# Linear attention, 32 heads: GpSimd sums the seven odd tiles 3 to 15 of phi(k) instead of tiles 10 to 14, and takes its relu of k whole, behind the memset of ones

## Chip, core and metric

The kernel runs on one core of one Trainium2 chip. The metric is the device time of one execution in microseconds (us); a smaller time is better.

## What is computed

There are 32 heads; in each, q, k and v are 2048 x 128 in bf16. Cut to what matters:

```python
phi_q = where(q > 0, q + 1, exp(q)) + 1e-6
phi_k = where(k > 0, k + 1, exp(k)) + 1e-6
kv  = einsum("bhsd,bhse->bhde", phi_k, v)      # 128 x 128 a head
z   = einsum("bhsd->bhd", phi_k)
num = einsum("bhqd,bhde->bhqe", phi_q, kv)
den = einsum("bhqd,bhd->bhq", phi_q, z)[..., None] + 1e-6
return num / den
```

The kernel writes phi(x) as a sum of two parts, min(exp(x), 1) + 1e-6 and max(x, 0). A matrix product with phi can so be made as two products, one with each part, that add up in PSUM, or as one product when some engine has added the parts before.

## The kernel before

**Data of a head.** The 2048 rows of a head are 16 tiles of 128 rows; partition p holds rows 16p to 16p + 15, and tile j is the 128 columns from 128 j. k, v and q come in by one 512 KB transfer each on SP's queue (L380) into six buffers each, and the output leaves by one (L590). `emk` (L401) and `emq` (L487) are the min-exp parts, `rk` (L391) and `rq` (L473 on ScalarE, L475 on VectorE) the relu parts; each has three buffers.

**Work of each engine for one head h in the steady part (h from 3 on).**

- ScalarE: exp of k (`ek`, L387), exp of the transposed q (`eq`, L466), relu of half of the transposed q (L473), and the copy of the summed kv and z out of PSUM (`kvs`, L449).
- VectorE, in this order in each turn: the denominators of a head (`den`, L525), their reciprocals (L531), a last tile (L536) and the divisions (L543, twice), then the other half of relu of q (L475), `emk` (L401) and `emq` (L487).
- GpSimd, in this order in each turn: `add` (L409), which adds the `emk` part to `rk` in place for the tiles in `ADD`, so that `rk` holds phi(k) there; the first half of relu of k of the next head (L391, tiles 0 to 7); the memset of ones (L445); the second half of that relu (L391, tiles 8 to 15).
- TensorE, in this order in each turn: for one head the first 2 of 5 groups of the numerators (`num`, L502 and L503); then the odd tiles of kv (`kv2`, L447) of the next head; then the other 3 groups of `num`; then the transposes of q (L455) and the even tiles of kv (L440 and L442) of the head after that.

**How kv takes its tiles.** A tile in `ADD` takes one product, with `rk`, which then holds the sum; another takes two, one with `emk`, one with `rk` (L426 and L427). An even tile (other than 0) is 128 columns of v wide and has a product one column wide for z with it (L436, recorded at L339); an odd tile is 129 wide, because the memset of ones has by then written 1 into the column of v ahead of it, the last column of the even tile before (L445). So the memset of head h waits until TensorE has read the even tiles of h, and the odd tiles wait for the memset.

**What sets the order.** Each operation is added to a plan with an engine and a key; each engine runs its own in order of the key, and the plan turns reads and writes into waits on semaphores. The keys that matter here: `add` of head h stands on GpSimd at h + 0.5, the memset of h at h + 0.6 (L445), the relu of k of head h at h - 0.45 and h (L398 and L399). `add` of head h reads `emk` and `rk` of h, and by its argument `more` it also waits until `emq` of head h - 1 is done (L421), the operation that VectorE runs right after `emk` of h:

```python
add("pool", h + 0.5, ADD, "phik",
    more=[("emq", (h - 1) % 3)] + ([("phik", 1)] if h == 2 else []))
```

On TensorE the even tiles are two operations: the even tiles outside `ADD` (L440), and behind them the even tiles in `ADD` (L442), which wait for `add`. `num` waits until VectorE's divisions of the head before have freed its PSUM groups, the first two groups by the first division and the rest by the second. The relu of q on VectorE waits until ScalarE's `eq` of that head is done. Heads 0 to 2 are a start of their own: head 0 is summed on VectorE whole, head 1 on VectorE for its even tiles 4 to 14 (L416) and for the odd tiles in `ADD` (L417), and relu of k is one whole instruction for heads 0 and 2 on GpSimd and for head 1 on VectorE (L396).

Of the kernel before, what the change touches and what calls it, by code (L numbers as in the profile page):

```python
# [12 lines left out]
def _ap(base: bass.AP, elem_offset: int, dims):  # L13
    return bass.AP(base.tensor, base.offset + elem_offset, [list(base.ap[0])] + [list(d) for d in dims])
# [217 lines left out]
def bass_standalone__linear_attn_elu__prompt_kernel(  # L232
# [18 lines left out]
    LAST = NH - 1  # L251
    SLOW = {LAST - 3: (16, 48)}

    ADD = (10, 11, 12, 13, 14)
    EVEN, ODD = tuple(range(0, NT, 2)), tuple(range(1, NT, 2))
    MORE = (4, 6, 8, 10, 12, 14)
    GAP = 32
# [7 lines left out]
    with ExitStack() as es:  # L265
# [39 lines left out]
        pl = Plan()  # L305

        def rows(x, h):
# [11 lines left out]
                                                     base=0, pattern=[[-1, P]], channel_multiplier=1),  # L319
               reads=[("id0",)], writes=[("ident",)])  # L320
# [17 lines left out]
        def mm_held(pe, out_ap, rhs, stop, start=False):  # L338
            return pe.add_instruction(mybir.InstMatmult(  # L339
                start_tensor_calc=start, stop_tensor_calc=stop, ldweights=False, bass_skip_group_check=True,  # L340
                tile_position=(0, 0), tile_size=(P, P), name=nc.get_next_instruction_name(), engine=mybir.EngineType.PE,
                ins=[pe.lower_ap(rhs), pe.lower_ap(held[0])], outs=[pe.lower_ap(out_ap)]))
# [27 lines left out]
        for h in range(NH):  # L370
            def at(name, key, h=h):
                return place.get((name, h), h + key)

            bi, b2, b3, bo = h % NBI, h % 2, h % 3, h % NBO

            def load(name, buf, src, key, h=h, bi=bi):
                dst, rws = buf[:, bi], rows(src, h)
                if name == "v":
# [9 lines left out]
                   reads=[("k", bi)], writes=[("ek", b2)])  # L388
            def relu_k(eng, key, parts, h=h, bi=bi, b3=b3):
                c = slice(parts[0] * HALF, (parts[-1] + 1) * HALF)  # L390
                pl.add(eng, key, lambda e: e.tensor_scalar(rk_sb[:, b3, c], k_sb[:, bi, c], BIG, 0.0, op0=ALU.min, op1=ALU.max),  # L391
                       reads=[("k", bi)] + ([("rk", h - 1, 1)] if 0 < h < 3 else []),
                       writes=[(n, b3, p) for p in parts for n in ("rk", "rkx")] + [("phik", b3), ("phix", b3)], kind="rk")

            if h < 3:
                relu_k("dve" if h == 1 else "pool", at("rk", 0), (0, 1))  # L396
            else:
                relu_k("pool", h - 0.45, (0,))  # L398
                relu_k("pool", h, (1,))  # L399
            pl.add("dve", at("emk", -3 + 0.95),  # L400
                   lambda d, b2=b2, b3=b3: d.tensor_scalar(emk_sb[:, b3, :], ek_sb[:, b2, :], 1.0, EPS, op0=ALU.min, op1=ALU.add),  # L401
                   reads=[("ek", b2)], writes=[("emk", b3)], kind="emk")

            def add(eng, key, tiles, name, b3=b3, more=()):
                step = tiles[1] - tiles[0]

                def f(e):
                    a, b = (_ap(x[:, :, :], b3 * NT * D + tiles[0] * D, [[step * D, len(tiles)], [1, D]]) for x in (rk_sb, emk_sb))
                    return e.tensor_tensor(out=a, in0=a, in1=b, op=ALU.add)  # L409
                pl.add(eng, key, f, reads=[("emk", b3), ("rkx", b3, 0), ("rkx", b3, 1)] + list(more), writes=[(name, b3)], kind=name)  # L410

            if h == 0:
                add("dve", -2.04, range(NT), "phik")
                both_of, one_of = (), range(NT)
            elif h == 1:
                add("dve", -1.89, MORE, "phix")  # L416
                add("dve", -1.88, tuple(j for j in ADD if j in ODD), "phik")  # L417
                both_of, one_of = tuple(j for j in EVEN if j not in MORE), MORE
            else:
                add("pool", h + 0.5, ADD, "phik",  # L420
                    more=[("emq", (h - 1) % 3)] + ([("phik", 1)] if h == 2 else []))  # L421
                both_of, one_of = (tuple(j for j in EVEN if (j in ADD) == x) for x in (False, True))

            def kv(pe, tiles, start=False, stop=False, h=h, bi=bi, b3=b3, both_of=both_of):
                for j in tiles:
                    both = j in both_of or (j in ODD and j not in ADD and h > 0)  # L426
                    for src in (emk_sb, rk_sb) if both else (rk_sb,):  # L427
                        first, fin = start and j == tiles[0] and src is (emk_sb if both else rk_sb), stop and j == tiles[-1] and src is rk_sb
                        w = src[:, b3, j * D:(j + 1) * D]
                        l = j == 0 or (j in ODD and h > 0)  # L430
                        c = GAP + j * D
                        last = pe.matmul(kvz_ps[:, 1 - l:NC], lhsT=w, rhs=v_sb[:, bi, c - l:c + D], start=first, stop=fin,  # L432
                                         skip_group_check=True)
                        if not l:
                            held[0] = w
                            last = mm_held(pe, kvz_ps[:, 0:1], ones_sb[:, 0:1], fin)  # L436
                return last
            base = [("v", bi), ("vo", bi), ("ones",), ("vones",)]
            if h:
                pl.add("pe", at("kv", -1.2), lambda pe, kv=kv, t=both_of: kv(pe, t, start=True),  # L440
                       reads=[("emk", b3), ("rk", b3, 0), ("rk", b3, 1)] + base, writes=[("bankkv",)])
            pl.add("pe", at("kv", -1.199), lambda pe, kv=kv, t=one_of, f=h == 0: kv(pe, t, start=f, stop=f),  # L442
                   reads=[("phix" if h == 1 else "phik", b3)] + base + ([] if h else [("first",)]), writes=[("bankkv",)])
            if h:
                pl.add("pool", h + 0.6, lambda g, bi=bi: g.memset(_ap(vfull, bi * VW + GAP + D - 1, [[2 * D, NT // 2], [1, 1]]), 1.0),  # L445
                       reads=[("v", bi)], writes=[("vo", bi)], kind="vo")
                pl.add("pe", at("kv2", -0.2985), lambda pe, kv=kv: kv(pe, ODD, stop=True),  # L447
                       reads=[("phik", b3), ("emk", b3), ("rk", b3, 0), ("rk", b3, 1), ("v", bi), ("vo", bi)], writes=[("bankkv",)])
            pl.add("act", at("kvs", -0.95), lambda a, b3=b3: a.activation(kvs_sb[:, b3, :], kvz_ps[:, 0:NC], ACT.Copy),  # L449
                   reads=[("bankkv",)], writes=[("kvs", b3)], kind="kvs")  # L450
# [31 lines left out]
            else:  # L482
# [5 lines left out]
                   reads=[("eq", b2, 0), ("eq", b2, 1)], writes=[("emq", b3)], kind="emq")  # L488
# [106 lines left out]
            if h in SLOW:  # L595
# [4 lines left out]
                    reads=[("row", i)] + [("o", bo, p) for p in ("t", 0, 1, 2, 3, 4)], dma=("o", NBO + 1 + i))  # L600
# [38 lines left out]
```

## Time and profile before

| | us |
|---|---|
| median of 3 runs | 167.63 (167.09 to 167.91) |
| the profiled execution, its own time | 167.01 |
| its span in the profile | 165.7 |
| busy in the span: TensorE, VectorE, ScalarE, GpSimd | 156.2, 153.6, 155.2, 107.6 |
| DMA: moved, mean rate | 67.25 MB, 406 GB/s |

The span is the time from the first to the last record of the profile; the profiled execution's own time has 1.3 us around it (167.01 - 165.7). "Busy" counts the time in which an engine had an instruction under way. In the group lines, a line of the kernel, its engine and its operation are followed by the output, the inputs, the shapes, the count, the busy time and the mean of one in ns. A line of the timeline gives the start in us, the time taken in us, the engine and the instruction; successive instructions of one engine overlap a little in these records, so what an instruction costs its engine in a row is the step from its start to the start of the next. In the waits, the numbers are the total in us, how many times, and the longest.

### The profile page before, as it was taken

To read this page: it belongs to the slowest core of one execution; us is meant where nothing else is said; L and a number is where in the kernel's file an instruction comes from. 1 tells how busy PE (TensorE), PEld (TensorE's weight loads), DVE (VectorE), ACT (ScalarE), POOL (GpSimd) and SP (SyncE) were. 2 spreads that over 40 slices of the span, in tenths; PEclk is the share of its full clock that TensorE was granted. 3 is DMA by queue.
4 is the path that set the end of the run, shared out by engine and by line. 5 is a ranking of instruction groups with operands and counts; after the bars stand their busy time and mean duration, and the time that the engine had idled before them with its cause. 6 is when DMAs were issued, how large, how long until landed. Compare 5 with 4: busy or idle time off the path is not lost.

```text
span 165.7 us, 6280 instructions
## 1 busy us (share of the span) xinstructions
PE 156.2 (94%) x2819; PEld 145.5 (88%) x2453; DVE 153.6 (93%) x277; ACT 155.2 (94%) x143; POOL 107.6 (65%) x130
## 2 busy tenths in 40 slices
PE   7779999999999999999999999999999999999990
PEld 0359899999999999999999989999998999999980
DVE  3587999999999999999999999999999999999993
ACT  3979999999999999999999999999999999999693
POOL 2405787676768867676787767677876767788320
PEclk9999999999999999999999999999999999999999
DMA  5999999999999999999999999999999999999986
GB/s 195 363 419 417 415 415 419 411 411 412 419 420 418 419 419 417 422 418 419 417 421 418 419 420 414 424 416 422 417 421 418 419 419 419 424 415 422 414 344 272
DMA packets 18605, 67.25 MB, mean 406 GB/s; under 512 B 2082, under 2 KB 2210, under 8 KB 18594
## 3 DMA queue, kind: packets, MB, share of 16 engines
q1 hardware_dynamic: 18448, 66.63, 99.2%
q0 software_dynamic: 144, 0.49, 0.7%
q8 instruction: 5, 0.08, 0.2%
q14 instruction: 6, 0.05, 0.1%
q10 hardware_dynamic: 2, 0.00, 0.0%
HBM read 50.33 MB, written 16.81 MB: 405 GB/s over the span
## 4 chain that ended last, share of the span: by engine, by line
DVE 62%; PE 16%; POOL 12%; DMA 4%; issue 3%; ACT 1%; SPq 1%; DVEq 0%
DVE o_sb L543 21%; POOL rk_sb L409 12%; DVE rq_sb L475 12%; DVE emq_sb L487 10%; DVE emk_sb L401 10%; PE kvz_ps L432 6%; PE o_ps L502 5%; PE o_ps L503 5%; DMA k_sb<-in_k_dram 4%; DVE rden_sb L531 3%; DVE o_sb L536 3%; DVE den_sb L525 2%; ACT ek_sb L387 1%; SPq L380 1%; DVE rk_sb L409 0%
## 5 line engine op out<-in xcount | busy, mean ns | idle before, releaser
L432 PE MATMUL kvz_ps<-v_sb,rk_sb 128*128 128x129 bf16 (+1 forms) x512 | 67.0, 220 | 2.7 <-POOL rk_sb L409 0.8
L543 DVE TENSOR_TENSOR o_sb<-o_ps,rden_sb 128x768 bf16<-128x768 f32 (+2 forms) x62 | 67.8, 1134 | 0.0
L409 POOL TENSOR_TENSOR rk_sb<-rk_sb,emk_sb 128x640 bf16<-128x640 bf16 x30 | 41.9, 1397 | 39.4 <-DVE emq_sb L487 38.1
L391 POOL TENSOR_SCALAR rk_sb<-k_sb 128x1024 bf16<-128x1024 bf16 (+1 forms) x60 | 64.2, 1070 | 2.4 <-DMA k_sb<-in_k_dram 2.4
L502 PE MATMUL o_ps<-kvs_sb,emq_sb 128*128 128x129 bf16 (+1 forms) x536 | 65.2, 217 | 0.0
L503 PE MATMUL o_ps<-kvs_sb,rq_sb 128*128 128x129 bf16 (+1 forms) x536 | 64.4, 217 | 0.0
L387 ACT ACTIVATE ek_sb<-k_sb 128x2048 bf16<-128x2048 bf16 x32 | 61.0, 1907 | 2.6 <-DMA k_sb<-in_k_dram 2.6
L466 ACT ACTIVATE eq_sb<-xT_ps 128x2048 bf16<-128x2048 bf16 (+1 forms) x33 | 60.0, 1822 | 2.1 <-PE xT_ps L455 2.1
L432 PE MATMUL kvz_ps<-v_sb,emk_sb 128*128 128x129 bf16 (+1 forms) x338 | 53.3, 221 | 0.5 <-DVE emk_sb L401 0.3
L432 PEld LDWEIGHTS kvz_ps<-v_sb,rk_sb 128*128 128x128 bf16 x512 | 46.1, 98 | 7.5 <-POOL rk_sb L409 2.7
L502 PEld LDWEIGHTS o_ps<-kvs_sb,emq_sb 128*128 128x128 bf16 x536 | 51.2, 98 | 0.8 <-issue 0.5
L503 PEld LDWEIGHTS o_ps<-kvs_sb,rq_sb 128*128 128x128 bf16 x536 | 51.2, 98 | 0.0
L455 PEld LDWEIGHTS xT_ps<-ident,q_sb 128*128 128x128 bf16 x512 | 30.1, 98 | 5.2 <-DMA q_sb<-in_q_dram 4.2
L455 PE MATMUL xT_ps<-ident,q_sb 128*128 128x128 bf16 x512 | 34.0, 220 | 0.7 <-DMA q_sb<-in_q_dram 0.3
L432 PEld LDWEIGHTS kvz_ps<-v_sb,emk_sb 128*128 128x128 bf16 x338 | 32.5, 98 | 0.9 <-DVE emk_sb L401 0.5
L339 PE MATMUL kvz_ps<-ones_sb,rk_sb 128*128 128x1 bf16 x232 | 31.3, 165 | 0.0
L473 ACT ACTIVATE rq_sb<-xT_ps 128x1024 bf16<-128x1024 bf16 x30 | 30.9, 1030 | 0.0
L401 DVE TENSOR_SCALAR emk_sb<-ek_sb 128x2048 bf16<-128x2048 bf16 x32 | 22.0, 688 | 3.6 <-ACT ek_sb L387 3.6
L475 DVE TENSOR_SCALAR rq_sb<-xT_ps 128x1024 bf16<-128x1024 bf16 x34 | 23.2, 688 | 1.0 <-PE o_ps L503 1.0
L487 DVE TENSOR_SCALAR emq_sb<-eq_sb 128x2048 bf16<-128x2048 bf16 x32 | 22.1, 691 | 0.0
L339 PE MATMUL kvz_ps<-ones_sb,emk_sb 128*128 128x1 bf16 x121 | 19.9, 166 | 0.0
L449 ACT ACTIVATE kvs_sb<-kvz_ps 128x129 bf16<-128x129 f32 x32 | 9.0, 282 | 1.5 <-PE kvz_ps L432 0.9
(37 smaller groups left out, 51.6 us busy)
## 6 DMA issues: line engine op xcount, KB each, us to landing
k_sb<-in_k_dram SPq DMA_DIRECT2D x32, 512.0 KB, 14.9
q_sb<-in_q_dram SPq DMA_DIRECT2D x32, 512.0 KB, 15.1
v_sb<-in_v_dram SPq DMA_DIRECT2D x32, 512.0 KB, 15.1
out_dram<-o_sb SPq DMA_DIRECT2D x30, 512.0 KB, 15.3
out_dram<-o_sb SPq DMA_DIRECT2D x1, 288.0 KB, 2.7
out_dram<-o_sb SPq DMA_DIRECT2D x1, 224.0 KB, 2.6
out_dram<-o_sb SPq DMA_DIRECT2D x2, 12.0 KB
out_dram<-o_sb SPq DMA_DIRECT2D x2, 4.0 KB
```

What stands on the lines that cost most here:

```text
L339: return pe.add_instruction(mybir.InstMatmult(start_tensor_calc=start, stop_tensor_calc=stop, ldweights=False, bass_skip_group_check=True, ...
L387: lambda a, bi=bi, b2=b2: a.activation(ek_sb[:, b2, :], k_sb[:, bi, :], ACT.Exp),
L391: pl.add(eng, key, lambda e: e.tensor_scalar(rk_sb[:, b3, c], k_sb[:, bi, c], BIG, 0.0, op0=ALU.min, op1=ALU.max), reads=[("k", bi)] + ([( ...
L409: return e.tensor_tensor(out=a, in0=a, in1=b, op=ALU.add)
L432: last = pe.matmul(kvz_ps[:, 1 - l:NC], lhsT=w, rhs=v_sb[:, bi, c - l:c + D], start=first, stop=fin, skip_group_check=True)
L455: last = pe.transpose(xT_ps[:, j * P:(j + 1) * P], q_sb[:, bi, j * P:(j + 1) * P], ident[:])
L466: halves[part] = pl.add("act", key, lambda a: a.activation(eq_sb[:, b2, c], xT_ps[:, c], ACT.Exp), reads=both[part:part + 1] or both, writ ...
L475: f = lambda d: d.tensor_scalar(rq_sb[:, b3, c], xT_ps[:, c], 0.0, None, op0=ALU.max)
L487: lambda d, b2=b2, b3=b3: d.tensor_scalar(emq_sb[:, b3, :], eq_sb[:, b2, :], 1.0, EPS, op0=ALU.min, op1=ALU.add),
L502: pe.matmul(o_ap, lhsT=emq_sb[:, b3, t * P:(t + 1) * P], rhs=kvs_sb[:, b3, c0:c1], start=True, stop=False)
L503: return pe.matmul(o_ap, lhsT=rq_sb[:, b3, t * P:(t + 1) * P], rhs=kvs_sb[:, b3, c0:c1], start=False, stop=True)
L543: pl.add("dve", key, lambda d: d.tensor_tensor(out=o_sb[:, bo, 3 * g0:3 * g1, :].rearrange("p (a b) d -> p a b d", b=3), in0=_ap(full, bas ...
```

## The change

`ADD` is now all odd tiles but tile 1. The even tiles all take two products and none of them waits for `add`; of the odd tiles, 1 takes two and the other seven take one. GpSimd's `add` has 7 tiles of 128 columns, each one tile apart from the next, in place of 5 adjacent ones. The relu of k of a head is one instruction over all 2048 columns, and stands behind the memset of ones of the head before; its first half stood ahead of that memset. In the start, VectorE's second sum of head 1 has 7 tiles in place of 2.

```diff
-    ADD = (10, 11, 12, 13, 14)
+    ADD = (3, 5, 7, 9, 11, 13, 15)
...
             if h < 3:
                 relu_k("dve" if h == 1 else "pool", at("rk", 0), (0, 1))
             else:
-                relu_k("pool", h - 0.45, (0,))
-                relu_k("pool", h, (1,))
+                relu_k("pool", h, (0, 1))
...
             elif h == 1:
                 add("dve", -1.89, MORE, "phix")
-                add("dve", -1.88, tuple(j for j in ADD if j in ODD), "phik")
+                add("dve", -1.88, ADD, "phik")
                 both_of, one_of = tuple(j for j in EVEN if j not in MORE), MORE
             else:
                 add("pool", h + 0.5, ADD, "phik",
                     more=[("emq", (h - 1) % 3)] + ([("phik", 1)] if h == 2 else []))
-                both_of, one_of = (tuple(j for j in EVEN if (j in ADD) == x) for x in (False, True))
+                both_of, one_of = EVEN, ()
...
-            pl.add("pe", at("kv", -1.199), lambda pe, kv=kv, t=one_of, f=h == 0: kv(pe, t, start=f, stop=f),
-                   reads=[("phix" if h == 1 else "phik", b3)] + base + ([] if h else [("first",)]), writes=[("bankkv",)])
+            if one_of:
+                pl.add("pe", at("kv", -1.199), lambda pe, kv=kv, t=one_of, f=h == 0: kv(pe, t, start=f, stop=f),
+                       reads=[("phix" if h == 1 else "phik", b3)] + base + ([] if h else [("first",)]), writes=[("bankkv",)])
```

The order of GpSimd's instructions in a turn of the steady part is so

| before | after |
|---|---|
| add of h, 640 columns (waits for `emq` of h - 1) | add of h, 7 x 128 columns (waits for `emq` of h - 1) |
| relu of k of h + 1, columns 0 to 1023 | memset of ones of h (waits for TensorE's even tiles of h) |
| memset of ones of h (waits for TensorE's even tiles of h) | relu of k of h + 1, columns 0 to 2047 |
| relu of k of h + 1, columns 1024 to 2047 | |

## Prediction

> **What bounds the kernel now.** I read the busy row first, then the DMA rows, the waits, and last the timelines of VectorE and GpSimd in the steady part.
>
> ```profile
> PE 156.2 (94%) x2819; PEld 145.5 (88%) x2453; DVE 153.6 (93%) x277; ACT 155.2 (94%) x143; POOL 107.6 (65%) x130
> ```
> ```profile
> DMA  5999999999999999999999999999999999999986
> ```
> ```profile
> DVE 62%; PE 16%; POOL 12%; DMA 4%; issue 3%; ACT 1%; SPq 1%; DVEq 0%
> ```
> ```profile
> POOL rk_sb L409 <- DVE emq_sb L487: 38.1, 29, 1.5
> ```
>
> The reader is to see that four resources are full together (VectorE, ScalarE, TensorE, DMA), that only GpSimd has room, and that GpSimd's idle time is one wait: 1.3 us in every turn, for `emq`. The third line is the chain that ended last: 62% of it is VectorE, and 12% is GpSimd's add, which the even tiles in `ADD` wait for. A turn is the distance of two `emk`: the VectorE timeline has `emk` of head 3 at 19.79 and of head 31 at 153.21, so (153.21 - 19.79) / 28 = 4.765 us.
>
> GpSimd's timeline over one turn, and VectorE's in its second half:
>
> ```profile
> 92.57 1.40 POOL L409 TENSOR_TENSOR rk_sb<-rk_sb,emk_sb 128x640 bf16<-128x640 bf16 x1 [1.23 <-DVE emq_sb L487]
> 93.94 1.04 POOL L391 TENSOR_SCALAR rk_sb<-k_sb 128x1024 bf16<-128x1024 bf16 x1
> 94.92 0.13 POOL L445 MEMSET v_sb<- 128x8 bf16 x1
> 94.98 1.04 POOL L391 TENSOR_SCALAR rk_sb<-k_sb 128x1024 bf16<-128x1024 bf16 x1
> 97.36 1.40 POOL L409 TENSOR_TENSOR rk_sb<-rk_sb,emk_sb 128x640 bf16<-128x640 bf16 x1 [1.34 <-DVE emq_sb L487]
> ```
> ```profile
> 95.39 0.69 DVE L475 TENSOR_SCALAR rq_sb<-xT_ps 128x1024 bf16<-128x1024 bf16 x1
> 96.00 0.68 DVE L401 TENSOR_SCALAR emk_sb<-ek_sb 128x2048 bf16<-128x2048 bf16 x1
> 96.59 0.68 DVE L487 TENSOR_SCALAR emq_sb<-eq_sb 128x2048 bf16<-128x2048 bf16 x1
> ```
>
> GpSimd is finished at 96.02, just as `emk` starts at 96.00. It then rests through `emk` and `emq`. Today GpSimd's work lies almost wholly beside VectorE's operations that read PSUM (`den`, the divisions, `rq`), and beside neither of the two that read and write SBUF alone. The trace shows what happens when they meet, once, in the start:
>
> ```profile
> 13.20 1.89 POOL L391 TENSOR_SCALAR rk_sb<-k_sb 128x2048 bf16<-128x2048 bf16 x1
> ```
> ```profile
> 14.73 0.91 DVE L487 TENSOR_SCALAR emq_sb<-eq_sb 128x2048 bf16<-128x2048 bf16 x1
> 15.56 0.68 DVE L401 TENSOR_SCALAR emk_sb<-ek_sb 128x2048 bf16<-128x2048 bf16 x1
> ```
>
> This `emq` came under a whole relu of k. It took 0.91 where the group's mean is 0.691, and the step to the next start is 0.83 where it is 0.60 elsewhere. So it really began at 15.56 - 0.60 = 14.96, and that is 1.76 after the relu's start. The relu itself took 1.89, as did the only other whole one on GpSimd (at 4.12), beside which no `emk` or `emq` ran. VectorE gave way; GpSimd lost nothing. A second, small meeting agrees: a half relu started at 23.57, `emk` at 24.44 took 0.71 and `emq` came at 25.08, so `emk` really began at 24.48, or 0.91 into a relu of 1.04. Both times VectorE was let in 0.13 before the relu's recorded end.
>
> **The change, part by part.** Let T be the recorded start of an `emq`.
>
> - *Add.* Its start is T + 0.77 (92.57 - 91.81, 97.36 - 96.59). For 640 columns it costs GpSimd 1.36 (92.57 to 93.94, less 0.01). For 896 there is no row. Per column it is at most 1.397 / 640 = 2.18 ns, and if the add has the fixed part that the relu shows (1.04 for 1024, 1.89 for 2048, so 0.83 ns a column and 0.19 fixed), it is 1.89 ns. 256 more columns cost 0.48 to 0.56. I take 0.52: 1.88. That the tiles are apart is priced by the memset: 8 separate elements take 0.135, single-element memsets 0.10 to 0.116, so below 5 ns a piece, 0.04 for seven; the bounds are 1.84 to 1.96.
> - *Memset.* A step of 0.065 (94.92 to 94.98). It now stands right behind the add and waits for the even tiles; that wait is worked out under TensorE.
> - *Relu of k.* One of 1.89 in place of two steps of 0.98, less work on its own. But it now starts at T + 0.77 + 1.88 + 0.065 = T + 2.71 and holds VectorE off until T + 2.71 + 1.76 = T + 4.47.
> - *emk.* In turns with no wait it comes 4.08 to 4.09 after the `emq` before (87.12 to 91.20, 96.59 to 100.68). So it meets the relu and waits 0.39. Then `emq` follows 0.60 later, and the next add hangs on that `emq`. This closes a ring: 0.77 + 1.88 + 0.065 + 1.76 + 0.60 = **5.07 us** a turn, 5.03 to 5.15 with the bounds of the add. Against 4.765 that is +0.305.
> - *TensorE.* Pairs of an even tile step by 0.081, odd products by 0.057. Before: 14 odd products (0.80) and 27 + 11 instructions in all; after: 9 odd (0.52), 14 pairs and tile 0 (14 x 0.081 + 0.115 = 1.25 against 1.01). The sum is 0.04 less, and the wait for the add in the middle of the even tiles goes. What is late next: the odd tiles wait for add and memset (T + 2.71), but ahead of them stand two groups of `num`, which wait for the first division, some 2.45 after T (91.81 to 94.28), and take 0.8. So the odd tiles come at T + 3.25 and never wait. They end at T + 3.8, then three groups of `num` run 1.05 to about T + 4.85, 0.2 before the next T. Transposes (0.95) and even tiles (1.25, with 0.17 to drain) follow: done 2.2 after that T, 0.45 ahead of the add's end at 2.65. So the memset doesn't wait either, and this cover of 0.45 is what rival 3 takes away.
> - *ScalarE* needs 4.68 to 4.79 a turn (`eq` at 83.94, 88.62, 93.41), *DMA* 4 x 0.524 MB a head; both get slack at 5.07. The k loads on SP wait for the relu, which now ends about 1 us later in a turn; they take 15 us to land with six buffers of 5 us each, so nothing hangs on it.
> - *Start.* VectorE's second sum of head 1 grows by 5 tiles, (1.224 - 0.286) / 1792 a column, +0.33; it would end at 12.9, ahead of `rq` at 13.53, which waits anyway, and of the odd tiles at 13.74. Nothing. The first add starts at 16.33 as before, so relu of head 3 at 18.28 lets `emk` in at 20.04 in place of 19.79: +0.25.
> - *End.* Behind the last relu, VectorE's own order sets the pace (div, `rq` at 157.27, `emq` at 158.53, no relu beside them). Nothing.
>
> **Sum:** 28 x 0.305 + 0.25 = 8.8 us. The profiled execution took 167.01, so **175.8**; by the bounds 174.6 to 178.1. The median of the runs is 0.6 above that execution, which the range takes in.
>
> Where the rule says more than the row: the Trainium skill, "SBUF — State Buffer", section "Who interferes with whom", has VectorE in a 2-port mode and GpSimd share one pair of ports, held by whoever comes first for the whole instruction. The trace agrees that the second one waits (0.91 against 0.69), but had it let in 0.13 before the recorded end; with the recorded end as the release, the ring would be 5.20 and the time 179.4. I hold to the row.
>
> **Rivals.**
>
> 1. *No wait worth speaking of* (the 0.91 was a thing of the start). For it: one clear row only. Then VectorE and ScalarE run at their own 4.68, TensorE's wait for the add gone: 28 x (4.68 - 4.765) = -2.4. But the DMA row is 9 from the third slice, and only the last two (344 and 272 GB/s of 418, a lack of 0.53 slices of 4.14 us) can give 2.2. So 164.8 to 167.0, not slower. It decides if `emk` under the relu stays below about 0.8. Chance 0.08.
> 2. *GpSimd gives way instead*: the relu stops when `emk` comes and goes on behind `emq`. GpSimd's round is then 1.88 + 0.065 + 1.76 + 1.2 = 4.9, 5.0 with a start: 28 x 0.185 = +5.2, **172.2**. Against it: both whole relus took 1.89. Chance 0.07.
> 3. *The memset waits for TensorE*, or the spaced tiles cost more than the memset shows: each 0.1 us beyond the cover goes straight into the ring, 2.8 us in all. With 0.2 it is 181. For it: even tiles without `add` are 0.24 longer and lie ahead of the memset; against it: the 0.45 above. Chance 0.09.
>
> My forecast keeps 0.76. A change of 0.5% is about what a measurement of this kernel can tell from none. The range reaches down to rival 2 and up past the bounds with the median's 0.6: 171.8 to 178.8. Faster 0.05, within 0.5% 0.04, slower 0.91.
>
> **What would show it.** VectorE's `emk` (L400 after the change) near 1.07 in place of 0.69 on average, its busy time up by about 11 us; `emk` to `emk` at 5.07; add near 1.9, relu 1.89, memset right behind the add with no wait for TensorE; ScalarE and TensorE with new idle time; the DMA row below 9 in places. I am wrong if `emk` stays at 0.69, if the relu stretches, or if the memset shows waits in the steady part.

## The result and the profile after

The changed kernel takes 173.98 us (median of 4 runs, 173.05 to 174.06) against 167.38 us for the kernel before (4 runs by now, 167.09 to 167.91): a ratio of 1.0375, 95% interval 1.0333 to 1.0416. Its profiled execution took 174.06, with a span of 172.8, 7.1 more than before.

First the page of the changed kernel: the busy row, the DMA rows, the chain that ended last by engine and by line, and the groups of `add` and relu of k on GpSimd and of `emk` on VectorE (line numbers below the edit are one lower than before).

```profile
PE 154.1 (89%) x2844; PEld 143.1 (83%) x2388; DVE 161.8 (94%) x277; ACT 156.2 (90%) x143; POOL 117.7 (68%) x101
...
DMA  5999999999999999999999999999999999996066
GB/s 212 352 418 422 413 418 416 409 417 416 416 421 421 415 421 420 418 418 416 419 420 419 420 419 417 420 419 420 419 419 421 419 419 422 418 417 275 18 231 252
...
DVE 79%; issue 13%; DMA 4%; ACT 1%; SPq 1%; PE 1%; DVEq 0%
DVE o_sb L543 25%; DVE emk_sb L400 17%; DVE rq_sb L475 13%; DVE emq_sb L487 11%; DVE rden_sb L531 6%; DVE o_sb L536 5%; DMA k_sb<-in_k_dram 4%; DVE den_sb L525 2%; ACT ek_sb L387 1%; SPq L380 1%; PE kvz_ps L431 0%; DVE rk_sb L408 0%; PE o_ps L502 0%; PE o_ps L503 0%; DVEq L220 0%
...
L408 POOL TENSOR_TENSOR rk_sb<-rk_sb,emk_sb 128x896 bf16<-128x896 bf16 x30 | 56.4, 1879 | 36.9 <-DVE emq_sb L487 35.7
...
L391 POOL TENSOR_SCALAR rk_sb<-k_sb 128x2048 bf16<-128x2048 bf16 x31 | 58.7, 1894 | 2.4 <-DMA k_sb<-in_k_dram 2.4
...
L400 DVE TENSOR_SCALAR emk_sb<-ek_sb 128x2048 bf16<-128x2048 bf16 x32 | 32.2, 1007 | 3.6 <-ACT ek_sb L387 3.6
```

The reader is to see one group that does the same work and takes longer: `emk`, 688 ns on average before, 1007 now. That is 10.2 us of VectorE's time (32.2 - 22.0), booked as busy, so VectorE's share looks as good as ever (94%). And the chain, which had 12% of GpSimd's add before, has no GpSimd at all now and 79% VectorE, although nothing was added to VectorE in the steady part. A chain follows waits between instructions; this wait lies inside one.

One turn of the changed kernel, GpSimd's timeline and then VectorE's:

```profile
96.75 1.88 POOL L408 TENSOR_TENSOR rk_sb<-rk_sb,emk_sb 128x896 bf16<-128x896 bf16 x1 [1.23 <-DVE emq_sb L487]
98.57 0.13 POOL L445 MEMSET v_sb<- 128x8 bf16 x1
98.64 1.89 POOL L391 TENSOR_SCALAR rk_sb<-k_sb 128x2048 bf16<-128x2048 bf16 x1
101.76 1.88 POOL L408 TENSOR_TENSOR rk_sb<-rk_sb,emk_sb 128x896 bf16<-128x896 bf16 x1 [1.23 <-DVE emq_sb L487]
```
```profile
95.99 0.68 DVE L487 TENSOR_SCALAR emq_sb<-eq_sb 128x2048 bf16<-128x2048 bf16 x1
...
99.44 0.68 DVE L475 TENSOR_SCALAR rq_sb<-xT_ps 128x1024 bf16<-128x1024 bf16 x1
100.04 1.04 DVE L400 TENSOR_SCALAR emk_sb<-ek_sb 128x2048 bf16<-128x2048 bf16 x1
101.00 0.68 DVE L487 TENSOR_SCALAR emq_sb<-eq_sb 128x2048 bf16<-128x2048 bf16 x1
```

The ring can be read off: `emq` at 95.99, add at 96.75 (0.76), memset at 98.57 (1.82), relu at 98.64 (0.07), `emk` let in at 101.00 - 0.60 = 100.40 (1.76 after the relu's start), next `emq` at 101.00 (0.60): 5.01 us. `rq`, which reads PSUM, ran under the same relu and took 0.68 as always. From `emk` of head 3 (19.96) to that of head 31 (160.19) a turn is 5.008 us; before it was 4.765. 28 x 0.243 = 6.8 of the 7.1 us.

The waits of the changed kernel (in total, times, longest):

```profile
POOL rk_sb L408 <- DVE emq_sb L487: 35.7, 29, 1.2
...
PE o_ps L502 <- DVE o_sb L543: 10.0, 28, 0.4
POOL v_sb L445 <- PE kvz_ps L339: 7.3, 1, 7.3
ACT kvs_sb L449 <- PE kvz_ps L431: 6.9, 27, 0.3
```

TensorE no longer waits for GpSimd at all; it now waits for VectorE's division in 28 turns, and ScalarE waits for TensorE in 27. The memset waited for TensorE once, in the start. Waits for the DMA stand in the start alone, at most two for any line.

### The profile page after: what moved, and what is told of

Same layout as the page of the kernel before. It is cut to its first block, busy times and chain, and to the rows that moved or that the text cites. A ratio compares the mean times of both kernels' runs of the same rounds, so it can differ in the third digit from the quotient of the medians.

```text
span 172.8 us, 6185 instructions
## 1 busy us (share of the span) xinstructions
PE 154.1 (89%) x2844; PEld 143.1 (83%) x2388; DVE 161.8 (94%) x277; ACT 156.2 (90%) x143; POOL 117.7 (68%) x101
## 2 busy tenths in 40 slices
DMA packets 18605, 67.25 MB, mean 389 GB/s; under 512 B 2082, under 2 KB 2210, under 8 KB 18594
## 4 chain that ended last, share of the span: by engine, by line
DVE 79%; issue 13%; DMA 4%; ACT 1%; SPq 1%; PE 1%; DVEq 0%
DVE o_sb L543 25%; DVE emk_sb L400 17%; DVE rq_sb L475 13%; DVE emq_sb L487 11%; DVE rden_sb L531 6%; DVE o_sb L536 5%; DMA k_sb<-in_k_dram 4%; DVE den_sb L525 2%; ACT ek_sb L387 1%; SPq L380 1%; PE kvz_ps L431 0%; DVE rk_sb L408 0%; PE o_ps L502 0%; PE o_ps L503 0%; DVEq L220 0%
## 5 line engine op out<-in xcount | busy, mean ns | idle before, releaser
L408 POOL TENSOR_TENSOR rk_sb<-rk_sb,emk_sb 128x896 bf16<-128x896 bf16 x30 | 56.4, 1879 | 36.9 <-DVE emq_sb L487 35.7
L431 PE MATMUL kvz_ps<-v_sb,rk_sb 128*128 128x129 bf16 (+1 forms) x512 | 62.0, 220 | 1.1 <-DVE rk_sb L408 1.1
L391 POOL TENSOR_SCALAR rk_sb<-k_sb 128x2048 bf16<-128x2048 bf16 x31 | 58.7, 1894 | 2.4 <-DMA k_sb<-in_k_dram 2.4
L431 PE MATMUL kvz_ps<-v_sb,emk_sb 128*128 128x128 bf16 (+1 forms) x273 | 46.6, 218 | 0.8 <-issue 0.4
L431 PEld LDWEIGHTS kvz_ps<-v_sb,rk_sb 128*128 128x128 bf16 x512 | 40.6, 97 | 2.6 <-DVE rk_sb L408 2.1
L339 PE MATMUL kvz_ps<-ones_sb,rk_sb 128*128 128x1 bf16 x232 | 36.4, 166 | 0.0
L400 DVE TENSOR_SCALAR emk_sb<-ek_sb 128x2048 bf16<-128x2048 bf16 x32 | 32.2, 1007 | 3.6 <-ACT ek_sb L387 3.6
L339 PE MATMUL kvz_ps<-ones_sb,emk_sb 128*128 128x1 bf16 x211 | 34.6, 166 | 0.0
L431 PEld LDWEIGHTS kvz_ps<-v_sb,emk_sb 128*128 128x128 bf16 x273 | 26.4, 97 | 1.3 <-DVE emk_sb L400 1.1
```

The costliest lines, as they stand in the source:

```text
L339: return pe.add_instruction(mybir.InstMatmult(start_tensor_calc=start, stop_tensor_calc=stop, ldweights=False, bass_skip_group_check=True, ...
```

## The experiments

Each ratio is to runs of the kernel before made along with it: their median is 167.17 us for the first four experiments and 167.41 us for the others. In brackets is the 95% interval. A turn is measured as before, from `emk` of head 3 to that of head 31.

**The new tiles alone.** The relu of k goes back to two halves, around the memset:

```diff
-                relu_k("pool", h, (0, 1))
+                relu_k("pool", h - 0.45, (0,))
+                relu_k("pool", h, (1,))
```

> The changed kernel with the relu of k in halves again, the first half ahead of the memset (so the new set of tiles alone). Theory (VectorE's emk stands still until GpSimd's relu lets it in, and the next add hangs on the emq behind it): from an emq's start, 0.76 to the add, 1.82 the add, 0.98 the first half, 0.065 the memset, 0.91 until the second half lets emk in, 0.60 to the next emq: 5.13 us a turn, 0.125 more than the 5.008 of the changed kernel, so about 177.5. Rival A (the cost is the whole relu behind the memset): as before the change, 167.4. Rival B (the cost is the new split of tiles on TensorE and the longer add, through TensorE): as after, 174.

Measured: 178.19 us, ratio 1.0638 (1.0568 to 1.0709), a turn of 5.158. Two lines of GpSimd's timeline and two of VectorE's:

```profile
97.03 1.04 POOL L391 TENSOR_SCALAR rk_sb<-k_sb 128x1024 bf16<-128x1024 bf16 x1
99.30 1.88 POOL L409 TENSOR_TENSOR rk_sb<-rk_sb,emk_sb 128x896 bf16<-128x896 bf16 x1 [1.23 <-DVE emq_sb L488]
```
```profile
97.42 1.20 DVE L401 TENSOR_SCALAR emk_sb<-ek_sb 128x2048 bf16<-128x2048 bf16 x1
98.54 0.68 DVE L488 TENSOR_SCALAR emq_sb<-eq_sb 128x2048 bf16<-128x2048 bf16 x1
```

`emk` really began at 98.54 - 0.60 = 97.94, 0.91 into the half relu, as the ring has it. So the whole relu behind the memset is not what costs: without it the new tiles are slower still, by 0.15 a turn. Of that, 0.13 is the second relu instruction (0.98 and 0.91 until `emk` is let in, against 1.76), and 0.02 is the add, whose step is 1.84 ahead of a relu. TensorE's odd tiles wait for the memset too in this run (13.8 us in 29 turns), but `emk` is let in 0.90 to 0.91 after the half relu's start in every turn, so the ring explains the turn without that wait.

The runs also tell a standstill from a slower pace. `emk` records its usual 0.68 and the time from its issue until it is let in: 1.04 and 0.36 in the changed kernel, 1.20 and 0.52 here. However long the two meet, it is let in 0.13 ahead of the relu's recorded end; had `emk` run on slowly beside the relu, a longer meeting would have moved that point.

**The new order alone.** The kernel before, with its tiles 10 to 14, and the whole relu behind the memset:

```diff
-                relu_k("pool", h - 0.45, (0,))
-                relu_k("pool", h, (1,))
+                relu_k("pool", h, (0, 1))
```

> The kernel before with the relu of k whole and behind the memset (the new order alone; tiles 10 to 14 as before). Theory: the add ends 2.12 after the emq's start, TensorE's three even tiles that wait for it take 0.24 and 0.2 to drain, the memset comes at 2.65, the relu at 2.7 and lets emk in at 4.46: 5.06 us a turn and about 175.5, although the add is as short as before. Rival A: about 174, as after. Rival B (longer add, new split): 167.4.

Measured: 176.97 us, ratio 1.0553 (1.048 to 1.0627), a turn of 5.109: 0.05 a turn more than expected. GpSimd's timeline, one of its waits, and VectorE's timeline:

```profile
93.45 1.40 POOL L408 TENSOR_TENSOR rk_sb<-rk_sb,emk_sb 128x640 bf16<-128x640 bf16 x1 [1.23 <-DVE emq_sb L486]
95.36 0.13 POOL L444 MEMSET v_sb<- 128x8 bf16 x1 [0.52 <-PE kvz_ps L339]
95.43 1.89 POOL L391 TENSOR_SCALAR rk_sb<-k_sb 128x2048 bf16<-128x2048 bf16 x1
```
```profile
POOL v_sb L444 <- PE kvz_ps L339: 23.3, 31, 7.4
```
```profile
96.74 1.14 DVE L400 TENSOR_SCALAR emk_sb<-ek_sb 128x2048 bf16<-128x2048 bf16 x1
97.80 0.68 DVE L486 TENSOR_SCALAR emq_sb<-eq_sb 128x2048 bf16<-128x2048 bf16 x1
```

Here the add is as short as before, and the memset is late for another reason: it waits 0.52 to 0.58 in each turn for the even tiles that themselves wait for the add. In the kernel before, the first half relu lies in that gap. So the two parts of the change belong together, each alone is slower than both, and in all three cases it is the relu's end that `emk` waits for (here 97.80 - 0.60 = 97.20, 1.77 after the relu's start).

**Six and five tiles.** The changed kernel with fewer odd tiles in the add:

```diff
-    ADD = (3, 5, 7, 9, 11, 13, 15)
+    ADD = (5, 7, 9, 11, 13, 15)
```

> The changed kernel with six odd tiles (5 to 15) in the add. Theory: the add is 0.24 shorter, the ring 4.77 us, as long as a turn before the change: 167 to 168. emk's mean falls to 0.75 or less. Rival A (the place of the relu) and rival B (TensorE's split): 173 to 174, since neither changes but for one tile.

Measured with six: 167.23 us, ratio 1.0000 (0.9968 to 1.0033), a turn of 4.776, `emk` 795 ns. With five (`ADD = (7, 9, 11, 13, 15)`):

> The changed kernel with five odd tiles (7 to 15) in the add. Theory: the ring is 4.53 us, below the 4.68 that VectorE and ScalarE need by themselves, so emk no longer waits (0.69) and the turn is theirs or DMA's: 165 to 167.4. Rivals A and B: 173 to 174.

Measured with five: 167.68 us, ratio 1.0023 (0.9996 to 1.0051), a turn of 4.788, `emk` 807 ns. The groups of the add and of `emk` with six, then with five, and one wait with five:

```profile
L408 POOL TENSOR_TENSOR rk_sb<-rk_sb,emk_sb 128x768 bf16<-128x768 bf16 x30 | 49.1, 1636 | 36.9 <-DVE emq_sb L487 35.7 <-DVE emk_sb L400 1.2
L400 DVE TENSOR_SCALAR emk_sb<-ek_sb 128x2048 bf16<-128x2048 bf16 x32 | 25.4, 795 | 3.6 <-ACT ek_sb L387 3.6
```
```profile
L408 POOL TENSOR_TENSOR rk_sb<-rk_sb,emk_sb 128x640 bf16<-128x640 bf16 x30 | 41.9, 1395 | 37.3 <-DVE emq_sb L487 36.0 <-DVE emk_sb L400 1.3
L400 DVE TENSOR_SCALAR emk_sb<-ek_sb 128x2048 bf16<-128x2048 bf16 x32 | 25.8, 807 | 3.1 <-ACT ek_sb L387 3.1
```
```profile
POOL v_sb L445 <- PE kvz_ps L339: 12.2, 30, 6.3
```

One tile less takes 0.24 off the add and 0.23 off the turn (5.008 to 4.776), and all of the loss is gone: the place of the relu is as in the changed kernel, and TensorE's order too but for that tile. `emk` still waits for the relu in every turn, so its mean is 0.80 and not the 0.75 or less expected. With five the expectation failed: `emk` did not return to 0.69, and the time is above the 165 to 167.4 given. TensorE has two more odd products than in the changed kernel, comes later with its even tiles, and the memset waits for it in 29 turns behind the start, 0.17 to 0.24 in the timeline. What the add gives up, that wait puts back, and the ring stays at 4.79. The timeline has no wait of a TensorE product from 30 to 150 us in this run, so I read TensorE's own work as the limit there; no run tries that.

**Half of the relu left out.** From head 6 on the relu covers columns 0 to 1023 only:

```diff
-                relu_k("pool", h, (0, 1))
+                relu_k("pool", h, (0, 1) if h < 6 else (0,))
```

> The changed kernel where, from head 6 on, GpSimd's relu of k covers only columns 0 to 1023; the other half of that relu is left out. The add, the memset, the tiles and TensorE's work stay. Theory: the relu lets emk in 0.91 after its start, the ring is 0.76 + 1.82 + 0.07 + 0.91 + 0.60 = 4.16 us, below the 4.68 that VectorE and ScalarE need, so emk is back at 0.69 and 26 turns give back up to 0.33 each: 165 to 167.5, with DMA full. Rival (the longer add, or the new order of TensorE's tiles, costs by itself): stays near 174.

Measured: 167.65 us, ratio 1.0013 (0.9981 to 1.0045); `emk` 713 ns on average (0.68 where the relu is half), a turn of 4.65 in the steady part (`emk` at 90.51, 95.16 and 99.81). The add with seven tiles and TensorE's order are untouched here, so neither of them costs anything by itself as long as the ring has room; in the ring, each column of the add counts, as the run with six tiles shows. The 4.65 is also what VectorE takes for a turn without a wait, a little less than the 4.68 that I had for it. VectorE had its last `emk` at 151.00, 2.2 us ahead of the kernel before (153.21), and the time is not shorter. Where that went, the page shows in its DMA rows:

```profile
DMA  5999999999999999999999999999999999999993
GB/s 209 361 414 420 416 420 412 408 396 413 418 420 419 419 419 418 420 420 414 419 420 419 419 419 416 419 420 419 418 421 418 419 421 419 418 421 418 414 412 143
```

DMA is full to the last slice but one. 67.25 MB at the 420 GB/s of a full slice are 160 us, and the first two slices and the last make up the rest. So I read the DMA as the floor here, and a faster turn does not bring this kernel clearly below the kernel before. For the same reason the times between 167 and 168 do not rank the versions; their turns do. The time came out just above the 165 to 167.5 expected.

**The add without its wait for `emq`.** The add's inputs are `emk` and `rk`; the wait for `emq` only orders it in time.

```diff
-                    more=[("emq", (h - 1) % 3)] + ([("phik", 1)] if h == 2 else []))
+                    more=[("phik", 1)] if h == 2 else [])
```

> The changed kernel without the add's extra wait for emq (the add needs emk and rk alone). VectorE issues emq right behind emk. Theory, whoever comes first keeps the other out: emq is first, so the add now waits inside its own record (about 0.4 more than 1.88), but starts the moment emq is through, 0.1 to 0.16 earlier than by the semaphore: 4.85 to 4.91 us a turn, 169.5 to 171. If instead the add gets in ahead of emq, emq is held off by 1.8 and the turn goes to some 6.6: over 200. If the two do not hinder each other there, the add ends 0.6 earlier: 4.7, about 167.

Measured: 167.88 us, ratio 1.0005 (0.9973 to 1.0037), a turn of 4.792. VectorE's timeline and GpSimd's:

```profile
92.21 0.82 DVE L400 TENSOR_SCALAR emk_sb<-ek_sb 128x2048 bf16<-128x2048 bf16 x1
92.95 0.68 DVE L487 TENSOR_SCALAR emq_sb<-eq_sb 128x2048 bf16<-128x2048 bf16 x1
```
```profile
93.11 2.25 POOL L408 TENSOR_TENSOR rk_sb<-rk_sb,emk_sb 128x896 bf16<-128x896 bf16 x1 [0.63 <-DVE emk_sb L400]
95.31 0.13 POOL L445 MEMSET v_sb<- 128x8 bf16 x1
95.38 1.89 POOL L391 TENSOR_SCALAR rk_sb<-k_sb 128x2048 bf16<-128x2048 bf16 x1
```

Now GpSimd is the one held off: the add is issued 0.16 into `emq`, takes 2.25 in place of 1.88, and `emq` keeps its 0.68. The add really begins at 95.31 - 1.82 = 93.49, 0.54 after the start of `emq`, where by the semaphore it began 0.76 after in the changed kernel. The gain is 0.22 a turn, more than the 0.10 to 0.16 that I expected, and the time is below the 169.5 to 171 given. The mechanism is the first of the three. Of the other two, an add ahead of `emq` would have shown in `emq`, and no hindrance at all in an add of 1.88.

**The whole relu ahead of the memset.**

```diff
-                relu_k("pool", h, (0, 1))
+                relu_k("pool", h - 0.45, (0, 1))
```

> The changed kernel with the whole relu of k ahead of the memset of ones. Theory of the VectorE ring alone: 0.07 less, 4.94 us a turn, 172. But the memset now comes 4.5 after the emq's start and TensorE's odd tiles, due at 3.25, wait for it; odd tiles 0.52, three groups of num 1.05 and their end make den ready at 6.4, and from den to the emq after it VectorE needs 4.08: 10.5 for two turns, 5.24 each, 180.5. So the wait for the memset should show on TensorE, 1.3 us a turn, and ScalarE's kvs behind it.

Measured: 181.38 us, ratio 1.0831 (1.0777 to 1.0884), a turn of 5.280. Three of its waits:

```profile
PE kvz_ps L431 <- POOL v_sb L445: 17.8, 29, 1.2
ACT kvs_sb L449 <- PE kvz_ps L431: 15.1, 29, 0.9
DVE den_sb L525 <- PE o_ps L503: 13.2, 29, 0.7
```

Here `emk` is free and VectorE stands still ahead of `den`, with TensorE waiting for the memset: another ring, through TensorE. Time and turn are near the 180.5 and 5.24 expected, but TensorE's wait is 0.6 a turn on average (17.8 / 29), half of the 1.3 that I gave: part of the lateness shows ahead of `den` instead, 0.46 a turn. This is what the place of the relu behind the memset avoids.

**Six tiles without the wait for `emq`,** both edits together:

> Six odd tiles (5 to 15) and no extra wait of the add for emq. Theory: the ring is 0.1 to 0.16 below the 4.776 of six tiles with the wait, so at or below the 4.68 of VectorE and ScalarE: emk near 0.69 to 0.72. The time can fall only as far as DMA lets it, which was full in six tiles with the wait: 165.5 to 167.3. If the add gets in ahead of emq: over 190.

Measured: 167.43 us, ratio 1.0009 (0.998 to 1.0038), a turn of 4.766, `emk` 789 ns, so not the 0.69 to 0.72 expected, and the time is just above the 165.5 to 167.3. `emk` takes 0.69 and 0.90 by turns: in 15 turns, every other one, the memset waited for TensorE (0.24 to 0.27). No version here beats the kernel before.

## Why the prediction was right

- *GpSimd's relu holds `emk` off, and the next add hangs on the `emq` behind it.* Right, and shown: with the relu halved the loss is gone while add and tiles stay; with one tile less the turn falls by what the add loses. `emk` took 1.04 (median), against the 1.07 I gave.
- *The ring of 5.07 us.* It is 5.008. The term that was off is the add: I took a step of 1.88, with 1.84 as the lower bound, and it is 1.82. The recorded 1.879 is just what the fixed part and 1.89 ns a column gave; but the memset starts 0.06 ahead of the add's recorded end, where the relu, from which I had the step, starts 0.04 ahead. 28 x 0.06 = 1.7 us, nearly all of the distance from 175.8 to the profiled execution's 174.06. That execution and the median of 173.98 lie below the 174.6 that the bounds gave: the range holds the result only because I had stretched it down to rival 2.
- *The release 1.76 into the relu, from one row of the start.* It held in each turn (1.75 to 1.77), and 0.91 into a half relu. There was more evidence than I had named: the small meeting of head 4 in the kernel before comes again at heads 10, 16, 22 and 28, where `emk` took 0.71 or 0.72 and was let in 0.90 to 0.92 after the half relu's start. The Trainium skill ("SBUF — State Buffer", "Who interferes with whom") says that whoever issues first keeps the other out for the whole instruction. The runs agree in both directions (`emk` behind the relu, the add behind `emq`), but the end that counts is 0.13 ahead of the recorded one; the reading by the recorded end, 179.4, is off.
- *Start and end at +0.25 and nothing.* The first `emk` was let in at 20.80 - 0.60 = 20.20, 0.41 later than before, of which 0.18 was there ahead of the first add (`emk` of head 2 at 15.74, before at 15.56): 0.23 from the relu. The 0.18 is a load of k that landed later (VectorE's first relu began at 9.32 in place of 9.14, with a wait for it); VectorE's longer second sum cost nothing, since `rq` behind it still waited 0.59. The end, from `emk` of head 31 as it began, took 12.2 in place of 12.5. VectorE's part of it is the same (9.83 and 9.84); the last two stores land in 2.4 and 2.3 us in place of 2.7 and 2.6. DMA is nearly empty shortly before (18 GB/s in a slice); that the stores land sooner for it is my reading and wasn't tried.
- *The odd tiles and the memset never wait.* Right in the changed kernel. That the cover is thin is shown with five tiles, where the memset waits in each turn, and by the new order alone, where it waits 0.52.
- *Rival 1* (no wait) and *rival 2* (GpSimd gives way) are out: all whole relus took 1.89 to 1.90. It is this row that excludes rival 2, and not the time: its 172.2 stands for a round of 4.95, and with the round of 5.0 that I named beside it the sum is 173.6, close to what was measured. Rival 1's second half holds, and stricter than I priced it: with the relu halved, DMA keeps the time at 167.65, and that run got nothing of the 2.2 us that I left for the end.
- *Each turn's loss counted in full in the time.* The sum takes this for granted, and it came out: 6.8 of the 7.1 us. It needed the kernel before to be paced by its turns and not by the DMA, and by the run with half the relu it was just at that edge: there a turn shorter by 0.11 gave nothing.
- *What would show it.* VectorE's busy time rose by 8.2 us, not 11: `emk` by 10.2, but other steps became shorter (from `emq` to `den` 0.66 to 0.60 on average, from the divisions to `rq` 2.17 to 2.13). That is also why the turn grew by 0.24 only, while `emk` waits 0.36: the kernel before lost some 0.11 a turn in such small waits, and they are gone. DMA fell below 9 only in the last four slices, not in places throughout: at 5.008 us a turn the 4 x 0.524 MB of a head are still 419 GB/s, what a full slice moves, so the lack shows only when the loads have run out.

## What to carry to other kernels

When an engine's idle time is moved, ask which instructions of the neighbour it lay beside, not only how long it was: GpSimd had 1.3 us a turn to spare, but just there VectorE ran the two operations that it cannot share with. Look for one place in the trace where the two meet, the start or the end of the kernel often has one; the length of the instruction that was held off, less its usual length, is the wait, and the next start behind it says when it was let in. A wait of this kind reads as busy time and leaves the engine that causes it out of the chain, so compare the mean of one instruction with that of the same instruction elsewhere.

## What the runs showed of the hardware that I had not expected

- An add queued behind `emq` without a semaphore began 0.54 us after the start of `emq`, one that waits for the semaphore 0.76 after: to let the two collide was 0.22 cheaper than to order them.
- GpSimd's add takes 1395, 1636 and 1879 ns for 640, 768 and 896 columns: 1.89 ns a column and 0.185 us fixed. Tiles spaced one apart cost the same as adjacent ones (1395 spaced, 1397 before).
